# The order of the last block's products, the place of block 0's projection, and the pace of attention tiles 4 to 7 in a fused sliding-window attention and SwiGLU kernel

## The chip, the core and the metric

The kernel runs on one core of a Trainium2 chip. The core has five engines with a queue each: PE (TensorE, matrix products), DVE (VectorE), ACT (ScalarE), POOL (GpSimd, here only an issuer of loads) and SP (SyncE, an issuer of DMAs). They run side by side and meet only at semaphores. Matrix products go from the on-chip memory SBUF into eight accumulator banks, PSUM, of 2 KB per partition; DVE and ACT read them out. Sixteen DMA engines move data between SBUF and the chip's main memory, HBM.

The metric is the device time of one execution in microseconds (us), less is better. A time is the median of several runs. A profile is one execution recorded instruction by instruction; its span runs from the first to the last recorded instruction.

## What is computed

There are 8 batches, 8 heads, 576 tokens and head size 64. Attention is causal with a window of 128 tokens and a linear penalty by distance. Its output, 4608 rows of 512, goes through a gated feed-forward part with 1536 hidden columns:

```python
scores = scale * np.matmul(q, k.transpose(0, 1, 3, 2))
mask = (rel >= 0) & (rel < window)              # window = 128
scores = np.where(mask, scores + bias[None], -1e9)
attn = np.exp(scores - np.max(scores, -1)); attn = attn / (np.sum(attn, -1) + 1e-9)
x = np.matmul(attn, v)          # (8, 8, 576, 64), regrouped to (4608, 512)
g = x @ w_gate
silu = g * (1.0 / (1.0 + np.exp(-g)))
out = (silu * (x @ w_val)) @ w_out
```

## The kernel before

**Attention** works on units: 36 tiles of 128 tokens by all 8 heads, nine for each pair of batches (`units`, line 160). For a tile, `scores` multiplies keys by queries into PSUM (L271, or L306 for the narrow form at the end of a batch), ACT takes the exponential (L277, L310), DVE multiplies with the mask (L283, L314), `weighted` multiplies with the values (L338), DVE divides by the sum (L340, L341) into a tile `x`, and `x_transposed` turns it into `xT` (L364 on PE with a copy on ACT at L368, or a DMA transpose from tile 24 on). Keys and queries are turned by `transposed` (L214, copies on ACT at L217 and DVE at L219) or, from rank 11 on, by a DMA issued from SP (L235). `attention` (L634) is a generator: the scores of tile i+1 are handed out in front of the weighting of tile i, and every `yield` is one attention step; a full tile has nine.

**The feed-forward part** works on nine blocks of 512 rows. For each of twelve hidden slices m, `gate_val` multiplies xT with the gate weights (pg, four matmuls of 512 columns at L390), ACT takes tanh (L404), DVE makes u = (tanh + 1) * pg (L405); then the same with the value weights (pv), and DVE multiplies into hT (L412). The PSUM tiles pg and pv rotate through three banks (`ps_f`, tag "gv"); attention's tiles rotate through four banks (`ps_a`, tag "a"); one more bank (`ps_f`, tag "po") is left for projections.

**The output product** of block 0 is made straight (`project`, L431: four row groups of 12 matmuls at L436, the result scaled on ACT at L440 and stored). For blocks 1 to 8 it is made by a Strassen-like scheme with seven products in place of eight (`strassen`, L481): per row group t (0 or 1) seven products of six matmuls of 256 columns (L502), which accumulate in two 256-column halves X and Y of one PSUM bank, and a separate tile p2. They need sums of quarters of hT (`sums`, L468) and of the weights (`weight_sums`, L453), made on DVE. Each `yield` in `strassen` follows one product. Between products ACT halves X or Y into `p1s`, `u2s`, `p5s`, and DVE finishes the four quarters of the result in `top` and `low`. `store` (L426) issues the DMA of a result from SP; for block 8, whose two half tiles of 64 rows lie in different batches, it issues two, and with `two` the second from ACT.

**The order.** `ffn` (L542) is a generator of feed-forward steps, with their size in steps as its value. `everything` (L709) walks through it, and in front of every step decides how many attention steps to hand out: as many as the running target says (`n_att < target`), and in any case until the tiles that the coming block needs are complete (`done < ready[blk]`; block 1 needs `ready[1] = 8` tiles, that is tiles 4 to 7). In step numbers, block 0 fills steps 1 to 24, block 1 with block 0's projection steps 25 to 60, and each later block 34.5 steps. Attention of tiles 0 to 3 and the first eight steps are put down in program order; behind that a scheduler of the language places the instructions, led by the order in which they were handed out and by its own idea of when each can start. So what is handed out earlier tends to stand earlier, without being bound to.

The last block has nothing beside it: its two row groups `ends[0]` and `ends[1]` are stepped by turns at L569.

Of the kernel before, what the change touches and what calls it, by code (L numbers as in the profile page):

```python
# [10 lines left out]
FP32 = mybir.dt.float32  # L11
# [5 lines left out]
P = 128  # L17
# [4 lines left out]
ALONE = 8  # L22
# [7 lines left out]
LEAD = 6  # L30
PRE = 0
SECOND = 5.5
# [15 lines left out]
def kernel(  # L48
# [10 lines left out]
    nc = tc.nc  # L59
    B, H, S, D = q.shape  # L60
    NTOK, DM = out.shape
# [79 lines left out]
    ps_f = ctx.enter_context(tc.tile_pool(name="ps_f", bufs=3, space=PSUM))  # L141
    ps_a = ctx.enter_context(tc.tile_pool(name="ps_a", bufs=4, space=PSUM))

    def busy(n):

        t_ = ps_f.tile([P, 512], FP32, name="nil", tag="po", bufs=1)
        for _ in range(n):
            nc.tensor.matmul(t_, idle[:, 0:P], idle, start=True, stop=True)
# [265 lines left out]
    def gate_val(n, m):  # L414
        c0 = 384 if (n, m) in acted else 0
        gate(n, m, wide(n, m, "g"), c0)
        yield
        val(n, m, wide(n, m, "v"), c0)
        yield

    def rows_of(n, j):
        if n == 8:
            return [(0, 64, 2 * j * S + 512), (64, 128, (2 * j + 1) * S + 512)]
        return [(0, 128, n * S + j * P)]

    def store(n, j, osb, c0=0, c1=512, two=False):  # L426
        for i, (p0, p1, r0) in enumerate(rows_of(n, j)):
            (nc.scalar if two and i else nc.sync).dma_start(out[r0:r0 + p1 - p0, c0:c1],
                                                            osb[p0:p1, c0:c1])

    def project(n, j, pool, tag, bufs):  # L431
        po = pool.tile([P, DM], FP32, name="po", tag=tag, bufs=bufs)
        for m0 in range(0, NMB, 4):
            for i in range(m0, m0 + 4):
                m = NMB - 1 - i if n == 0 else i
                nc.tensor.matmul(po, hT[n][:, m, j * P:(j + 1) * P], wo_sb[:, m, :],  # L436
                                 start=(i == 0), stop=(i == NMB - 1))
            if m0 + 4 == NMB:
                osb = opool.tile([P, DM], FP32, name="osb", tag="osb")
                nc.scalar.mul(osb, po, 0.5)  # L440
                store(n, j, osb)
            yield
# [5 lines left out]
    HC = DM // 2  # L448
    T1, T2, T3, T4 = (consts.tile([P, HM, HC], FP16, name=f"T{n}") for n in (1, 2, 3, 4))
# [3 lines left out]
    def weight_sums(c):  # L453

        if c == 0:
            one_more.append(supool.tile([P, 1], FP32, name="one", tag="pin", bufs=1))
            nc.vector.memset(one_more[0], 1.0)
        k = slice(2 * c, 2 * c + 2)
        for t_, a, b in ((T1, B12, B11), (T3, B22, B12)):
            nc.vector.scalar_tensor_tensor(out=t_[:, k, :], in0=a[:, k, :], scalar=one_more[0],  # L460
                                           in1=b[:, k, :], op0=ALU.mult, op1=ALU.subtract)
        nc.vector.tensor_sub(T2[:, k, :], B22[:, k, :], T1[:, k, :])
        nc.vector.tensor_sub(T4[:, k, :], B21[:, k, :], T2[:, k, :])
# [17 lines left out]
    def strassen(n, t):  # L481

        h = hT[n]
        A11, A12 = h[:, 0:HM, 0:256], h[:, HM:NMB, 0:256]
        S1, A22 = h[:, 0:HM, 256:512], h[:, HM:NMB, 256:512]
        S2, S3, S4 = hsum[n]
        cols = slice(t * P, (t + 1) * P)
        end = n == NBLK - 1
        pool, tag, bufs = (ps_a, "a", 4) if end and t else (ps_f, "po", 1)
        po = pool.tile([P, 2, HC], FP32, name="po", tag=tag, bufs=bufs)  # L490
        p2 = ps_a.tile([P, HC], FP32, name="p2", tag="a")
        top, low = (opool.tile([P, DM], FP32, name="osb", tag="osb") for _ in range(2))
        if end and t:
            spare = [opool.tile([P, DM], FP32, name="osb", tag="osb") for _ in range(2)]
            p1s, p5s, u2s = spare[0][:, 0:HC], spare[0][:, HC:DM], spare[1][:, 0:HC]
        else:
            p1s, p5s, u2s = (supool.tile([P, HC], FP32, name=i, tag=i, bufs=1)
                             for i in ("p1s", "p5s", "u2s"))

        def product(dst, a, b, start=False):  # L500
            for m in range(HM):
                nc.tensor.matmul(dst, a[:, m, cols], b[:, m, :], start=(start and m == 0),  # L502
                                 stop=(m == HM - 1), skip_group_check=True)

        def half_plus(dst, a, b):
            nc.vector.scalar_tensor_tensor(out=dst, in0=a, scalar=0.5, in1=b,
                                           op0=ALU.mult, op1=ALU.add)

        X, Y = po[:, 0, :], po[:, 1, :]
        product(X, A11, B11, True)  # L510
        nc.scalar.mul(p1s, X, 0.5)
        yield
        product(p2, A12, B21, True)
        half_plus(top[:, 0:HC], p2, p1s)
        yield
        product(X, S2, T2)
        nc.scalar.mul(u2s, X, 0.5)
        yield
        product(Y, S1, T1)
        nc.scalar.mul(p5s, Y, 0.5)  # L520
        yield
        product(X, S3, T3)
        half_plus(low[:, HC:DM], X, p5s)
        if end and t:
            store(n, t + 2, low, HC, DM, True)
        yield
        product(Y, S4, B22)
        half_plus(top[:, HC:DM], Y, u2s)
        store(n, t, top, 0, DM, end)
        yield  # L530
        product(X, A22, T4)
        if end:
            nc.vector.tensor_scalar_mul(low[:, 0:HC], X, 0.5)
        else:
            nc.scalar.mul(low[:, 0:HC], X, 0.5)
        store(n, t + 2, low, 0, HC if end and t else DM, end)
        yield
# [4 lines left out]
    def ffn():  # L542

        for n in range(NBLK):
            if n > 1:
                parts = chain(strassen(n - 1, 0), strassen(n - 1, 1))
            if n == 1:
                for j in range(PRE):
                    for _ in project(0, j, ps_f, "po", 1):
                        yield 1.0  # L550
            for m in range(NMB):
                for half, _ in enumerate(gate_val(n, m)):
                    yield 1.0
                    if n > 1 and 2 * m + half in AT:
                        next(parts)
                        yield 0.75
                if n == 1:
                    if m in (3, 5, 7, 9):
                        for _ in project(0, m // 2 - 1, ps_f, "po", 1):
                            yield 1.0  # L560
                    if m in (4, 6, 8):
                        weight_sums(m // 2 - 2)
                if n > 0 and m >= 9:
                    sums(n, m - 9)
            if n > 1:
                assert next(parts, None) is None

        ends = [strassen(NBLK - 1, t) for t in range(2)]
        for t in 7 * (0, 1):  # L569
            next(ends[t])  # L570
            yield 0.75

# [130 lines left out]
    def progress(steps):  # L703
        total = 0.0
        for size in steps:
            total += size
            yield total

    def everything():  # L709
        nonlocal done  # L710
        base = 0
        busy(WARM)
        with tc.manual_schedule(engines=ENGINES[MANUAL]):
            first_tiles()
            done = FIRST
            steps = progress(ffn())
            while (at := next(steps)) < ALONE:
                if at == 2.0:
                    nc.scalar.copy(idm2, idm)
                if at in (1.0, 3.0, 4.0):  # L720
                    later_masks(2 * (1, 3, 4).index(at) + 2, 2)
        for step in steps:
            if step == MASKS_AT:
                make_masks()

            b1 = 24 + 3 * PRE

            lead = LEAD if done < X_DMA_FROM - 2 else LEAD + 4
            blk = (0 if step + LEAD < b1 else 1 if step + LEAD < 60
                   else min(NBLK - 1, 2 + int((step + lead - 60) // 34.5)))  # L730
            if step < b1:

                target = base + 1.25 * max(0, step - ALONE) + 1.5 * max(0, step - 16)
            elif step < 60:
                target = base + 32 + SECOND * 8 * (step - b1) / (60 - b1)
            else:
                target = base + 32 + SECOND * 8 + (step - 60) * RATE * 8 / 34.5
            while (n_att < target or done < ready[blk]) and att_step():
                pass

    everything()


# [28 lines left out]
```

The softmax here doesn't subtract the row's maximum and nothing guards it: scores larger than these inputs give would overflow.

## Time and profile before

| what | value |
|---|---|
| median of 4 runs | 355.14 us (354.98 to 356.29) |
| the profiled execution, its own time | 354.98 us |
| its span | 353.2 us |
| granted TensorE clock, mean over the span | 0.997 |
| PE busy | 341.2 us of the span |
| DVE busy | 279.4 us |
| ACT busy | 178.1 us |
| matmuls of gate and value, L390 | 115.1 and 114.9 us |
| last twelve matmuls, L502 | 346.98 to 348.45 us |
| last PSUM read, L533 on DVE | 348.49 to 348.91 us |
| last store's issue ends | 349.62 us on SP, 349.92 us on ACT |

The busy time of PE is made of overlapping matmuls, so it says when the engine had something in flight and not that it ran at its peak. A finer measure is the distance between starts: four matmuls of 512 columns in a row take 0.86 us, and where the distance is longer, PE waited. The last 4.3 us of the span hold no matmul.

### The profile page before, as it was taken

To read this page: it belongs to the slowest core of one execution; us is meant where nothing else is said; L and a number is where in the kernel's file an instruction comes from. 1 tells how busy PE (TensorE), PEld (TensorE's weight loads), DVE (VectorE), ACT (ScalarE), POOL (GpSimd) and SP (SyncE) were. 2 spreads that over 40 slices of the span, in tenths; PEclk is the share of its full clock that TensorE was granted. 3 is DMA by queue.
4 is the path that set the end of the run, shared out by engine and by line. 5 is a ranking of instruction groups with operands and counts; after the bars stand their busy time and mean duration, and the time that the engine had idled before them with its cause. 6 is when DMAs were issued, how large, how long until landed. Compare 5 with 4: busy or idle time off the path is not lost.

```text
span 353.2 us, 7294 instructions
## 1 busy us (share of the span) xinstructions
PE 341.2 (97%) x2767; PEld 197.1 (56%) x2767; DVE 279.4 (79%) x619; ACT 178.1 (50%) x357; POOL 108.4 (31%) x134
## 2 busy tenths in 40 slices
PE   7999989999999999999999999999999999999994
PEld 4584444444466646565466555664665566456673
DVE  5568887998777798788986998799878965975772
ACT  2758774655655455565546455455444323332330
POOL 8976582439574365553301110000000000000000
PEclk9999999999999999999999999999999999999998
DMA  9999999999999999999945513211022101101004
GB/s 152 171 180 186 143 183 160 90 156 131 141 180 152 178 169 171 170 157 129 175 53 106 89 35 34 86 34 57 17 75 61 45 2 60 59 2 60 32 30 120
DMA packets 158819, 37.34 MB, mean 106 GB/s; under 512 B 147264, under 2 KB 154304, under 8 KB 158784
## 3 DMA queue, kind: packets, MB, share of 16 engines
q0 software_dynamic: 117280, 18.62, 82.7%
q1 hardware_dynamic: 40816, 17.57, 26.6%
q10 hardware_dynamic: 688, 0.69, 0.6%
q8 instruction: 21, 0.34, 0.4%
q14 instruction: 14, 0.11, 0.1%
HBM read 37.91 MB, written 9.44 MB: 134 GB/s over the span
## 4 chain that ended last, share of the span: by engine, by line
PE 80%; DVE 9%; ACT 7%; issue 2%; ACTq 0%; DVEq 0%
PE pv L390 23%; PE pg L390 23%; PE po L502 16%; PE av L338 4%; PE ps L271 4%; PE p L502 3%; DVE uu L405 2%; ACT exc L310 2%; PE px L364 2%; ACT ex L277 2%; DVE hT L412 2%; PE po L436 2%; ACT tt L404 2%; DVE ex L283 1%; PE pt L214 1%
## 5 line engine op out<-in xcount | busy, mean ns | idle before, releaser
L390 PE MATMUL pv<-xT,wv_sb 128*128 128x512 f16 (+2 forms) x464 | 114.9, 364 | 0.9 <-DVE uu L405 0.5
L390 PE MATMUL pg<-xT,wg_sb 128*128 128x512 f16 (+2 forms) x464 | 115.1, 364 | 0.3 <-DVE xT L366 0.2
L404 ACT ACTIVATE tt<-pg 128x512 f16<-128x512 f32 (+2 forms) x110 | 65.4, 594 | 91.4 <-PE pg L390 87.6
L405 DVE SCALAR_TENSOR_TENSOR uu<-tt,pg 128x512 f16<-128x512 f16 (+2 forms) x109 | 73.4, 674 | 33.0 <-ACT tt L404 32.5
L412 DVE TENSOR_TENSOR hT<-uu,pv 128x512 f16<-128x512 f16 (+2 forms) x110 | 74.0, 673 | 7.3 <-PE pv L390 3.3
L390 PEld LDWEIGHTS <-wv_sb 128*128 128x128 f16 x464 | 42.8, 98 | 37.8 <-issue 3.6
L390 PEld LDWEIGHTS <-wg_sb 128*128 128x128 f16 x464 | 42.7, 98 | 36.8 <-issue 2.8
L277 ACT ACTIVATE ex<-ps 128x512 f16<-128x512 f32 x96 | 50.3, 605 | 14.8 <-PE ps L271 14.8
L181 POOL DMA_DIRECT2D va<-in_v_dram x40 | 34.1, 860 | 45.6 <-PE av L338 37.1
L502 PEld LDWEIGHTS <-hT 128*128 128x128 f16 x384 | 36.4, 98 | 15.9 <-issue 3.4
L187 POOL DMA_DIRECT2D qn<-in_q_dram x39 | 33.3, 859 | 29.8 <-DMA qT<-qn 13.0
L187 POOL DMA_DIRECT2D kn<-in_k_dram x39 | 33.3, 858 | 25.4 <-DMA kT<-kn 21.4
L283 DVE TENSOR_TENSOR ex<-ex,m_reg 128x1024 f16<-128x1024 f16 x42 | 28.8, 688 | 8.2 <-ACT ex L277 8.1
L502 PEld LDWEIGHTS <-S 128*128 128x128 f16 x288 | 27.4, 98 | 12.3 <-issue 2.9
L341 DVE TENSOR_TENSOR x<-av,rec 128x256 f16<-128x256 f32 x72 | 29.2, 420 | 0.7
L502 PE MATMUL po<-T,S 128*128 128x256 f16 x192 | 26.0, 273 | 0.6 <-ACT p5s L520 0.6
L502 PE MATMUL po<-T,hT 128*128 128x256 f16 x192 | 26.1, 272 | 0.4
L310 ACT ACTIVATE exc<-psc 128x512 f16<-128x512 f32 x40 | 21.5, 612 | 4.8 <-PE psc L306 4.8
L338 PEld LDWEIGHTS <-ex 128*128 128x128 f16 x384 | 17.8, 97 | 5.1 <-issue 0.9
L338 PE MATMUL av<-va,ex 128*128 128x65 f16 x384 | 19.9, 193 | 0.4
L271 PE MATMUL ps<-qT,kT 64*128 64x256 f16 x192 | 17.9, 273 | 0.3 <-DVE qT L219 0.2
L368 ACT COPY xT<-px 128x512 f16<-128x512 f16 x20 | 11.7, 585 | 9.6 <-PE px L364 9.5
(82 smaller groups left out, 293.7 us busy)
## 6 DMA issues: line engine op xcount, KB each, us to landing
out_dram<-osb SPq DMA_DIRECT2D x32, 256.0 KB, 2.6
va<-in_v_dram POOLq DMA_DIRECT2D x32, 128.0 KB, 8.1
qn<-in_q_dram POOLq DMA_DIRECT2D x31, 128.0 KB, 7.2
kn<-in_k_dram POOLq DMA_DIRECT2D x31, 128.0 KB, 7.2
wo_sb<-in_moe_w_out_dram POOLq DMA_DIRECT2D x2, 768.0 KB, 9.0
wg_sb<-in_moe_w_gate_dram POOLq DMA_DIRECT2D x4, 256.0 KB, 7.8
wv_sb<-in_moe_w_val_dram POOLq DMA_DIRECT2D x4, 256.0 KB, 8.2
wg_sb<-in_moe_w_gate_dram POOLq DMA_DIRECT2D x1, 512.0 KB, 9.1
```

The costliest lines, as they stand in the source:

```text
L181: nc.gpsimd.dma_start(va[rank][p0:p1, :, 0:D], src)
L187: nc.gpsimd.dma_start(t_[p0:p1], src)
L271: nc.tensor.matmul(two[par][:, j, :], kT[rows, ks, pair, :], qT[rows, p:p + 2, pair, :], start=(j == 0 and not early_tile), stop=(j == 1))
L277: nc.scalar.activation(e[:, o:o + 2, :], banks[q4][par], AF.Exp, scale=scale)
L283: nc.vector.tensor_mul(e[:, o, :], e[:, o, :], reg[:, o, :])
L338: nc.tensor.matmul(av[:, j, :], w, val, start=(n == 0), stop=(n == len(todo) - 1))
L341: nc.vector.tensor_mul(x[:, 4 * half:4 * half + 4, :], av[:, :, 0:D], rec.broadcast_to([P, 4, D]))
L390: nc.tensor.matmul(ps[:, c0:c1], w[:, kb, ms], xT[n][:, kb, c0:c1], start=(kb == 0 and c0 == 0), stop=(kb == NKB - 1 and c1 == 512), skip_ ...
L404: nc.scalar.activation(tt, pg[:, c0:c1], AF.Tanh, scale=0.5)
L405: nc.vector.scalar_tensor_tensor(out=uu, in0=tt, scalar=one if (n, m) == PIN else 1.0, in1=pg[:, c0:c1], op0=ALU.add, op1=ALU.mult)
L412: nc.vector.tensor_mul(hT[n][:, m, c0:c1], acted[(n, m)][1][:, c0:c1], pv[:, c0:c1])
L502: nc.tensor.matmul(dst, a[:, m, cols], b[:, m, :], start=(start and m == 0), stop=(m == HM - 1), skip_group_check=True)
```

## The change

Three things are edited.

1. In the last block, X and Y get a PSUM bank each from the four of attention (`ps_a`), and p2 one of the three "gv" banks. Before, row group 0 had its X and Y in the "po" bank and row group 1 in a bank of `ps_a`. The order of the fourteen products is no longer by turns, but 0 1 0 1 0 0 0 1 0 0 1 1 1 1. Row group 1's upper result is stored in two halves of 256 columns, the first one straight behind its second product, both parts of it from SP; and row group 1's `p5s` is made on DVE in place of ACT.
2. In block 1, the four row groups of block 0's projection are handed out behind slices m = 4, 6, 8, 10 in place of 3, 5, 7, 9.
3. The target of attention steps up to step 24 rises by 1.6 a step from step 8 and 2.75 from step 16 (before 1.25 and 2.75), to 34.8 at step 24 in place of 32; from there it starts at 34 in place of 32 and meets the old line at step 60. And the rule that tiles 4 to 7 be complete takes effect one step ahead of block 1 (`step + 1 < b1`) in place of six.

```diff
@@ strassen
-        pool, tag, bufs = (ps_a, "a", 4) if end and t else (ps_f, "po", 1)
-        po = pool.tile([P, 2, HC], FP32, name="po", tag=tag, bufs=bufs)
-        p2 = ps_a.tile([P, HC], FP32, name="p2", tag="a")
+        if end:
+            X, Y = (ps_a.tile([P, HC], FP32, name="po", tag="a", bufs=4) for _ in range(2))
+            p2 = ps_f.tile([P, HC], FP32, name="p2", tag="gv")
+        else:
+            po = ps_f.tile([P, 2, HC], FP32, name="po", tag="po", bufs=1)
+            X, Y = po[:, 0, :], po[:, 1, :]
+            p2 = ps_a.tile([P, HC], FP32, name="p2", tag="a")
...
-        X, Y = po[:, 0, :], po[:, 1, :]
         product(X, A11, B11, True)
         nc.scalar.mul(p1s, X, 0.5)
         yield
         product(p2, A12, B21, True)
         half_plus(top[:, 0:HC], p2, p1s)
+        if end and t:
+            store(n, t, top, 0, HC)
         yield
         product(X, S2, T2)
         nc.scalar.mul(u2s, X, 0.5)
         yield
-        product(Y, S1, T1)
-        nc.scalar.mul(p5s, Y, 0.5)
+        product(Y, S1, T1, end)
+        if end and t:
+            nc.vector.tensor_scalar_mul(p5s, Y, 0.5)
+        else:
+            nc.scalar.mul(p5s, Y, 0.5)
...
         half_plus(top[:, HC:DM], Y, u2s)
-        store(n, t, top, 0, DM, end)
+        store(n, t, top, HC if end and t else 0, DM, end)
@@ ffn
-                    if m in (3, 5, 7, 9):
-                        for _ in project(0, m // 2 - 1, ps_f, "po", 1):
+                    if m in (4, 6, 8, 10):
+                        for _ in project(0, m // 2 - 2, ps_f, "po", 1):
                             yield 1.0
...
-        for t in 7 * (0, 1):
+        for t in (0, 1, 0, 1, 0, 0, 0, 1, 0, 0, 1, 1, 1, 1):
             next(ends[t])
@@ everything
-            blk = (0 if step + LEAD < b1 else 1 if step + LEAD < 60
+            blk = (0 if step + 1 < b1 else 1 if step + LEAD < 60
...
-                target = base + 1.25 * max(0, step - ALONE) + 1.5 * max(0, step - 16)
+                target = base + 1.6 * max(0, step - ALONE) + 1.15 * max(0, step - 16)
             elif step < 60:
-                target = base + 32 + SECOND * 8 * (step - b1) / (60 - b1)
+                target = base + 34 + (SECOND * 8 - 2) * (step - b1) / (60 - b1)
```

Here `LEAD` is 6, `ALONE` 8, `SECOND` 5.5, `b1` 24 and `base` 0.

## The prediction

> **What bounds the kernel now.** I read the page first, for the engines and their course over the span.
>
> ```profile
> PE 341.2 (97%) x2767; PEld 197.1 (56%) x2767; DVE 279.4 (79%) x619; ACT 178.1 (50%) x357; POOL 108.4 (31%) x134
> ...
> PE   7999989999999999999999999999999999999994
> ```
>
> PE is the bound, and its low slices are the first ones (before 18 us, where the change does nothing), the sixth (44 to 53 us) and the last. So an edit of order can win only what PE loses there. Next I read the busy time by stretches, with borders at what the change touches: the attention of tiles 4 to 8 up to block 1's first matmul at 56.11, block 1, and the end. Columns are the stretch, its length, then busy time of PE, PEld, DVE, ACT, POOL (with counts), clock, DMA share and GB/s.
>
> ```profile
> 36.00:44.00 8.00, 7.90 (x71) 3.92 (x69) 6.82 (x15) 5.67 (x12) 4.62 (x7) 1.00 2.05 139
> 44.00:47.50 3.50, 3.50 (x28) 1.78 (x26) 3.40 (x9) 2.11 (x5) 3.50 (x6) 1.00 1.22 184
> 47.50:55.50 8.00, 6.70 (x95) 3.99 (x95) 6.41 (x16) 6.15 (x14) 4.57 (x6) 1.00 1.81 180
> 60.00:70.00 10.00, 10.00 (x77) 4.76 (x76) 9.76 (x21) 5.69 (x11) 3.62 (x5) 1.00 1.46 99
> 70.00:80.00 10.00, 9.79 (x66) 4.37 (x65) 10.00 (x24) 6.27 (x12) 4.18 (x5) 1.00 1.91 156
> 349.00:353.20 4.20, 0.00 (x0) 0.00 (x0) 0.00 (x0) 0.00 (x0) 0.00 (x0) 0.73 0.52 170
> ```
>
> PE idles 1.30 us between 47.5 and 55.5 and next to nothing around it; DVE is full from 60 to 80; the last 4.2 us belong to the DMAs. The chain of waits inside that window says what PE waits for (start, length, what):
>
> ```profile
> 48.52 0.99 ACT exc L310 x2
> ...
> 49.53 0.69 DVE exc L314
> 50.22 0.16 DVE rec L340 x2
> 50.38 0.40 DVE x L341
> ...
> 50.83 0.28 PE px L364 x2
> 51.11 0.37 PE psc L306 x8
> 51.49 1.07 ACT exc L310 x2
> 52.56 0.48 ACT xT L368
> 53.04 1.00 ACT exc L310 x2
> ```
>
> This is the serial course of tiles 6, 7 and 8 through ACT and DVE, with hardly a feed-forward matmul between its steps: the old rule completes tiles 4 to 7 from step 18 on, and block 0 has little left to put between them. At the other end I read the DMA issues of the last stores, the first pair (window 346.2 to 347) and the last pair (349.0 to 349.3):
>
> ```profile
> out_dram<-osb SPq DMA_DIRECT2D x1, 64.0 KB, 2.0
> out_dram<-osb ACTq DMA_DIRECT2D x1, 64.0 KB, 2.3
> ...
> out_dram<-osb SPq DMA_DIRECT2D x1, 64.0 KB, 2.7
> out_dram<-osb ACTq DMA_DIRECT2D x1, 64.0 KB, 2.8
> ```
>
> The same 64 KB take 0.5 to 0.7 us longer in the last pair, because 1 MB is pressed into the DMA engines within 3 us.
>
> **The change part by part.** *Attention of tiles 4 to 8.* The built order of the changed kernel differs from the old one from 30.6 us (matmul 295 on each side) to matmul 811 (102.5 us before); behind that PE's order is the same up to the last block, so whatever is won or lost carries through. I laid the new order out by hand from 30.63 us, each instruction behind the one ahead of it, what it reads, and the read that frees its bank. Durations are from the timeline: 0.216 us for a matmul of 512 columns (four in 0.86), 0.22 for four transposes, 0.24 for a weighting half, 0.49 for an ACT exponential or copy, 0.61 for a DVE operation of 512 or a mask (0.68 less the overlap), 0.35 for L341, and 0.2 from a matmul group's end to its reader. What it gives:
> - Removed: in the old order one matmul (0.22 us) stands between tile 6's weighting and its transposes (px). That matmul should end at 50.00; px starts at 50.83 and, for the second half, at 51.76 in place of 51.23: 0.83 + 0.53 of waiting. In the new order eight matmuls stand there (1.73 us). The new chain is two mask operations, two reciprocals and two L341, ready some 2.4 us behind the first weighting half: a wait of about 0.4 is left, none for the second half.
> - Added: tile 5 loses that cover, four matmuls behind its weighting where there were nine. A tanh stands ahead of tile 6's exponentials, and the first weighting half needs the bank that the first of these frees: 0.5 more. Its x then comes late for px, and px's banks for the transposes behind: 0.2. Tile 5's own queries are copied behind one more DVE operation: 0.3.
> - The rest (scores of tile 8 and its weighting, which wait for ACT's copy and exponentials in both orders) I get at 0.75 now and 0.55 before.
>
> By this, block 1's first matmul comes at 55.75 in place of 56.11, with 10 of the projection's matmuls done in place of 8: 0.36 + 2 x 0.216 = **0.8 us won**. The bounds: no more than the idle PE of 36 to 55.5 in the rows plus the gaps too short for them (0.10 + 1.30 + about 0.3) = 1.7 won; and if the removed waits come back in full while the added ones stay, 1.0 lost. I take 0.8.
>
> *Block 0's projection.* The 48 matmuls (L436) are the same. The scheduler pulled the first ones into the attention of tile 8 already (matmul 479 before, 487 now). What moves is the rest: at matmul 680, 36 of them were done before and 32 are now, so 4 x 0.216 = 0.86 us of PE work without DVE is late, and one slice's DVE work comes earlier, while DVE is full (10.00 of 10.00). ACT's reads and SP's four stores move along; POOL's loads, which the new order also shuffles on POOL and SP, were ahead: the waiting lists hold no wait of PE for a load. PE idles 0.21 from 70 to 80, so 0.2 can be won; if the late 0.86 us is all waited for, 0.9 is lost. I take 0: pg and pv have three banks, worth 2.6 us of matmuls, as cover.
>
> *The last block.* Eighty-four matmuls at 109 ns are 9.16 us, and they take 9.3 (338.98 to the last nominal end at 348.29): 0.1 can be won. A product's reader ends 1.28 us behind its start, and PE goes on 0.06 later; two products last 1.31. In the old order every product waits for a read two products back, since X and Y share a tile. In the new one only three do (S3T3 of group 0, the last two of group 1, of which one reads `p5s` on DVE); S1T1 now stands alone. I take 0 here, bounds 0.1 won to 0.3 lost (three waits of 0.1).
>
> *The stores.* Before, 1 MB is issued from 346.28 to 349.16. Now a 128 KB half goes at about 342.3, group 0's two results at 345.6 and 346.3, and the last three halves 0.65 us apart. The issues cost SP and ACT about 0.55 each and stand 0.65 apart, so they don't pile up; the lanes that they reuse landed long before. The last pair (2.7 and 2.8) should then go towards the first pair (2.0 and 2.3): 2.8 - 2.35 = **0.45 won**, bounds 0 and 0.7. In the built program the last landing also moves from the third of SP's eight final waits to the fifth or sixth; these go by in 0.06 us each in the trace: **0.12 won**.
>
> The Trainium skill (DMA: Bandwidth & Descriptors, under "Measured (HBM→SBUF, 128 partitions, SWDGE, issued from GpSimd)") speaks against pieces like these: it asks for DMAs of 1 MiB and calls those under 64 KB bound by their descriptors. The row is against it here, since 64 KB landed after 2.0 us alone and 2.7 in the crowd. The page's own fit of 2.0 us plus bytes over 436 GB/s would make the last pair an estimated 2.15 us, and the gain 0.65 in place of 0.45.
>
> *Sum*, on the profiled execution (354.98 us, of which the span is 353.2 and 1.8 lie around it): 0.8 + 0 + 0 + 0.45 + 0.12 = 1.37, so 353.6. Its run lies 0.16 below the median of 355.14, so against the median I forecast **353.8 us**.
>
> **The rivals.** *Only the end gains.* The waits of tiles 6 to 8 move to tile 5 and to block 1 and PE ends where it did: 355.14 - 0.57 = 354.6. For it: ACT and DVE must do the same serial work, and my list of added waits is as long as that of the removed ones. Against it: DVE has 1.6 us free between 47.5 and 55.5 and another 1.2 between 36 and 44.
>
> *DVE in block 1 becomes the bound.* Place: 60 to 80 us, where DVE has 0.24 us free in 20. If the late projection and the attention steps that now stand in block 1's first slices put DVE further behind than the three banks cover (2.6 us), PE waits for every slice until DVE catches up behind 80. The price is the DVE work of two slices that arrive without cover, each L405 + L412 = 1.35: 2.7 us, less 0.57 at the end: 355.14 + 2.1 = 357.2; half of that gives 355.9. For it: the row with 10.00. Against it: the change leaves DVE's amount of work in block 1 nearly the same, and weight sums stay where they were.
>
> *The change doesn't do what it says.* The scheduler orders behind step 8, so a pace handed out need not be the pace built. The built order does show the spread (eight matmuls in place of one ahead of px), so I hold this for spent but for the projection, which hardly moves; it is within the first rival.
>
> **How the numbers follow.** The forecast case has 0.62, its own range 352.8 (both main bounds nearly full: 355.14 - 1.7 - 0.6) to 354.5. Only the end gains: 0.20. DVE becomes the bound: 0.18. About 0.3%, 1.07 us, is what a measurement tells from no change, so faster means under 354.07: most of the first case, 0.52, and 0.03 of the second; the same holds 0.10 of the first, 0.17 of the second and 0.02 of the third; slower the remaining 0.16. The range 352.7 to 355.8 takes in the first two cases and the milder part of the third.
>
> **What would show it.** Right: busy PE in the stretch before block 1 up by about 0.8 us, tile 6's px without a wait of 0.7, block 1's first matmul near 55.8, the seventh product's matmuls 0.8 us earlier than at 346.98, and last landings near 2.3 us after issue. Wrong: waits of PE for DVE between 60 and 80 us, tile 5's weighting waiting more than 0.7, or the last pair still at 2.7.

## The result, and the profile after

The changed kernel takes 355.06 us in the median of 52 runs; the kernel before, run beside it 77 times, takes 355.91. The ratio of the means is 0.9971, with a 95% interval of 0.9965 to 0.9978, or 1.03 us of 355.14. (The medians differ by 0.85 only, since the changed kernel's runs fall in two groups, see below.) So it is faster, by three quarters of the 1.37 us that the forecast had, and its 353.8 is 0.3 us too low on the old median (355.14 - 1.03 = 354.1). Three of the four runs shown before had been at the low end of the kernel's own spread.

The profiled execution took 355.06 us, its span is 353.285 (before 353.203 of 354.98). So this pair of profiles shows no gain at all, while 52 runs do. That is what has to be explained. First the busy shares and PE's forty slices on the page:

```profile
span 353.3 us, 7299 instructions
...
PE 341.0 (97%) x2767; PEld 197.9 (56%) x2767; DVE 279.3 (79%) x620; ACT 177.1 (50%) x356; POOL 108.4 (31%) x134
...
PE   7999998999999999999999999999999999999995
```

The sixth slice (44 to 53 us) is at nine tenths or more now, and the seventh (53 to 62) is at eight instead. The stretches say the same in microseconds (columns as in the prediction):

```profile
47.50:55.50 8.00, 7.01 (x82) 3.90 (x80) 6.40 (x16) 5.42 (x11) 4.62 (x6) 1.00 1.81 180
55.50:57.50 2.00, 1.15 (x10) 0.72 (x10) 0.61 (x2) 0.57 (x1) 0.88 (x1) 1.00 2.45 154
60.00:70.00 10.00, 10.00 (x76) 4.57 (x75) 9.84 (x22) 5.29 (x10) 4.08 (x5) 1.00 1.99 138
70.00:80.00 10.00, 10.00 (x68) 4.53 (x68) 9.98 (x22) 6.80 (x14) 6.70 (x10) 1.00 2.19 152
```

PE gains 0.31 us of busy time between 47.5 and 55.5 (6.70 before) and is idle for 0.85 of the next two (busy 1.15 of 2.00; 1.98 before). From 60 to 80 it is full beside a full DVE, so the rival of DVE did not come. The list of PE's waits from 30 to 58 us (total, times, longest) names the loser:

```profile
PE po L436 <- DMA wo_sb<-in_moe_w_out_dram: 1.1, 1, 1.1
PE ps L271 <- DVE qT L219: 0.5, 1, 0.5
PE av L338 <- ACT ex L277: 0.3, 1, 0.3
PE px L364 <- DVE x L341: 0.3, 1, 0.3
PE psc L306 <- ACT xT L368: 0.3, 1, 0.3
```

Before, the same list had px with 1.0 us in two waits and ps with 0.2, and nothing else. So one of px's two waits is gone and the other is smaller, as forecast; ps waits longer, two small waits (av, psc) are new, and one that was not forecast tops the list: block 0's projection waits for the second half of the output weights. The chain of waits over 48 to 58 us shows that wait as a load of 11 us, with PE behind it (start, length, what):

```profile
45.14 11.17 DMA wo_sb<-in_moe_w_out_dram
56.31 0.04 issue
56.35 0.38 PE po L436
...
57.71 0.45 PE pg L390 x2
```

The timeline of PE says what it cost, in starts: the matmul after 54.84 should stand at 55.06.

```profile
54.84 0.38 PE L436 MATMUL po<-wo_sb,hT 128*128 128x512 f16 x1
56.35 0.38 PE L436 MATMUL po<-wo_sb,hT 128*128 128x512 f16 x1 [1.13 <-DMA wo_sb<-in_moe_w_out_dram]
```

At the end the last stores land sooner (issues behind 349.65 us; the second ACT store there is the last to land, at 352.19):

```profile
out_dram<-osb ACTq DMA_DIRECT2D x2, 64.0 KB, 2.3
out_dram<-osb SPq DMA_DIRECT2D x1, 64.0 KB, 2.1
```

Three distances sum up the end. The last 84 matmuls take 9.08 us from first to last start in place of 9.19; from the last matmul's start to the last landing it is 3.26 us in place of 3.81; from there to the end of the span 1.09 in place of 1.22. Together 0.79 us.

### The profile page after: what moved, and what is told of

It reads as the page before. It is cut to its first block, busy times and chain, and to the rows that moved or that the text cites. A ratio compares the mean times of both kernels' runs of the same rounds, so it can differ in the third digit from the quotient of the medians.

```text
span 353.3 us, 7299 instructions
## 1 busy us (share of the span) xinstructions
PE 341.0 (97%) x2767; PEld 197.9 (56%) x2767; DVE 279.3 (79%) x620; ACT 177.1 (50%) x356; POOL 108.4 (31%) x134
## 4 chain that ended last, share of the span: by engine, by line
PE 72%; DMA 11%; DVE 6%; ACT 4%; POOL 4%; issue 3%; DVEq 0%; ACTq 0%; POOLq 0%
PE pv L390 21%; PE pg L390 21%; PE po L506 16%; DMA wg_sb<-in_moe_w_gate_dram 4%; PE av L338 4%; DMA wo_sb<-in_moe_w_out_dram 3%; DMA va<-in_v_dram 3%; PE p L506 3%; PE ps L271 3%; PE po L436 2%; DVE hT L412 2%; DVE uu L405 1%; ACT ex L277 1%; POOL va L181 1%; PE px L364 1%
```

## The experiments

In all runs the time outside the span is mostly 1.7 to 2.1 us, at times up to 3.5, whatever the kernel. So the spans of all runs (the profiled one included) are the finer measure, and they already say something: 23 runs of the changed kernel span 351.8 to 352.5 us, 30 span 353.0 to 354.3, and none lies between.

**The two halves of the change.** The first kernel has only the edits of `strassen` and of the order of the fourteen products, the second only those of `ffn`'s projection and of `everything`.

```diff
 tail_only
-            pool, tag, bufs = (ps_a, "a", 4) if end and t else (ps_f, "po", 1)
+            X, Y = (ps_a.tile([P, HC], FP32, name="po", tag="a", bufs=4) for _ in range(2))
...
-        for t in 7 * (0, 1):
+        for t in (0, 1, 0, 1, 0, 0, 0, 1, 0, 0, 1, 1, 1, 1):
 mid_only
-                    if m in (3, 5, 7, 9):
+                    if m in (4, 6, 8, 10):
...
-                target = base + 1.25 * max(0, step - ALONE) + 1.5 * max(0, step - 16)
+                target = base + 1.6 * max(0, step - ALONE) + 1.15 * max(0, step - 16)
```

> Only the last block's part of the change (banks, order of the fourteen products, half store, p5s on DVE); pace and projection as before. Theory A (the end gives its full gain whatever the middle does): the profile of the changed kernel shows 0.11 us less for the last 84 matmuls, 0.55 us less from the last matmul to the last landing, 0.13 us less behind it; so 0.79 us faster than the kernel before, ratio 0.9978, and both its fastest and its slowest runs shift alike. Rival B (the gain at the end was the smaller part, most of the 1.03 us came from the pace): 0.3 us or less, ratio 0.999 or above.

> Only the pace of tiles 4 to 7 and the later projection; the last block as before. Theory A: PE gains 0.4 us by the first product of block 1 where the second half of wo_sb is there in time, and nothing or a loss where PE waits for it as in the profile of the changed kernel (1.29 us between two projection matmuls at 54.84 us); so runs fall in two groups about 1.2 us apart as those of both kernels do, and the ratio is 0.9985 to 1.0005. Rival B: 0.8 us as forecast, ratio 0.9978.

The last block's part alone took 354.73 us, ratio 0.9975 (0.9958 to 0.9992); the middle alone 356.37, ratio 1.001 (0.9998 to 1.0022). So the last block's part brings the gain (theory A) and the middle, on this stream of loads, none. The spans of the middle alone fall in two groups about 1.4 us apart, three of twelve at 353.0 to 353.3 and nine at 354.2 to 355.0, as theory A had it. Both profiles wait for the weights. First the last block's part, then the middle alone, the top of each list of PE's waits:

```profile
PE px L364 <- DVE x L341: 1.0, 2, 0.7
PE po L436 <- DMA wo_sb<-in_moe_w_out_dram: 0.8, 1, 0.8
```

```profile
PE po L436 <- DMA wo_sb<-in_moe_w_out_dram: 1.5, 1, 1.5
PE ps L271 <- DVE qT L219: 0.4, 1, 0.4
```

The first of them has the old order of attention, whose profile before had no such wait. So the wait is not a thing of the new order alone.

**The weights one load earlier.** The load of `wo_sb[0:6]` is issued straight behind that of `wo_sb[6:12]`, ahead of the keys and queries of ranks 9 and 10, in both kernels.

```diff
     nc.gpsimd.dma_start(wo_sb[:, 6:12, :], wo2[:, 6:12, :])
+    nc.gpsimd.dma_start(wo_sb[:, 0:6, :], wo2[:, 0:6, :])
     load_qk(9)
     load_qk(10, "q")
-    nc.gpsimd.dma_start(wo_sb[:, 0:6, :], wo2[:, 0:6, :])
```

> The changed kernel with one load moved: the half of wo_sb that holds rows 0 to 5 is issued straight behind the other half, ahead of the keys and queries of ranks 9 and 10. The orders of PE, DVE and ACT are the same as in the changed kernel. Theory A (the late landing of this load parts the runs into two groups and takes back the gain in the middle): the wait of 1.29 us is gone, the runs are one group near the lower one, median 353.9, ratio to the kernel before 0.994 to 0.9955. Rival C (the two groups come from elsewhere, for instance from the first loads): two groups as now, ratio 0.997.

> The kernel before with the same load moved as in the run above it. Theory A: its two groups (near 355.2 and 356.2) become one near 355.1, ratio 0.997 to 0.9985, and the profile shows no wait of PE for wo_sb. Rival C: two groups as before, ratio 1.000. If A holds here and in the changed kernel, the difference of these two is the change without the load: 1.2 us.

The changed kernel so took 354.4 us (0.997, 0.9953 to 0.9986), ten of twelve spans at 352.3 to 352.8: the upper group is nearly gone, as theory A had it, but the lower one is 0.3 to 0.5 us higher, so the time is the one of rival C. Its profile waits for the queries of rank 10, which the weights now stand ahead of:

```profile
PE pt L214 <- DMA qn<-in_q_dram: 0.3, 1, 0.3
```

The kernel before took 356.25 (1.0016, 0.9999 to 1.0032): no gain, against theory A. The loads land one behind another (in the profile before, the three between the two halves of the weights landed 0.8 to 1.0 us apart), so in the changed kernel the move made another load the late one. For the kernel before that isn't shown: its profile (span 353.5) waits for no load, and why its spans stayed at 353.5 to 355.2, with one of 357.3, is open.

**Rank 8's values behind them.** What isn't needed soon is rank 8's values. In this edit both halves of the weights stand in front and the values behind rank 10's queries, in three kernels: changed, before, and the last block's part alone. The order of PE, DVE and ACT is each kernel's own.

```diff
-    load(8)
+    load_qk(8)
     nc.gpsimd.dma_start(wo_sb[:, 6:12, :], wo2[:, 6:12, :])
+    nc.gpsimd.dma_start(wo_sb[:, 0:6, :], wo2[:, 0:6, :])
     load_qk(9)
     load_qk(10, "q")
-    nc.gpsimd.dma_start(wo_sb[:, 0:6, :], wo2[:, 0:6, :])
+    load_v(8)
     load_v(9)
```

> The changed kernel with both halves of the output weights loaded right behind rank 8's queries and keys, and rank 8's values behind rank 10's queries (the order of the matmuls, of DVE and of ACT is the changed kernel's). Theory A (the middle wins about 0.4 us where loads are out of the way, and the changed kernel's two groups of spans come from the last part of the weights' second half): no wait of PE for the weights and none of more than 0.2 us for the queries of rank 10, since these keep their place; block 1's first matmul near 56.3 with the start of block 1 of the changed kernel's good runs, spans in one group at 352.0 or under, 3.1 us under the kernel before in the median of time it should show 0.995 to 0.996. Theory B (the middle wins nothing even so, the tail is all): the spans go to 352.5 to 353.0, as with the last block's part alone, and some other wait of 0.3 to 0.5 us takes the place of that for the weights.

> The kernel before with the same move of the loads. Theory A (the kernel before doesn't wait for its weights in most runs): 0.999 to 1.001, spans with a median of 353.8 to 354.1. Theory B (the broad spread of its spans, 353.1 to 354.8, is also made by late loads): the spread becomes narrow, 353.0 to 353.6, and the ratio 0.998.

> The last block's part of the change alone, with the same move of the loads. Theory A: span 0.8 us under that of the kernel before with this move (0.55 from the last matmul to the last landing, 0.13 behind it, 0.11 in the last 84 matmuls), and 0.4 us over the changed kernel with this move. Theory B: no difference to the changed kernel with this move (within 0.15 us).

| kernel, loads moved | median, us | ratio to before (95%) | spans, us |
|---|---|---|---|
| changed | 353.98 | 0.9945 (0.9927 to 0.9963) | 351.8 to 352.3 |
| last block's part alone | 354.48 | 0.9957 (0.9941 to 0.9973) | 352.1 to 353.3 |
| before | 355.57 | 0.9988 (0.9974 to 1.0002) | 353.2 to 353.9 |

Theory A holds for the changed kernel: it has one group of spans now, block 1's first matmul stands at 56.28, and at 0.9945 it is better than both kernels of this study. In its list of PE's waits the weights are gone and the other four are as they were:

```profile
PE ps L271 <- DVE qT L219: 0.4, 1, 0.4
PE av L338 <- ACT ex L277: 0.3, 1, 0.3
PE px L364 <- DVE x L341: 0.3, 1, 0.3
PE psc L306 <- ACT xT L368: 0.3, 1, 0.3
```

The spans of the kernel before went from 353.1 to 354.8 (median 354.1) to 353.2 to 353.9: its longer half is gone too, which speaks for theory B, though B had 353.6 as the upper end and the ratio's interval still holds 1. And the middle, which was worth nothing above, is now worth some: 0.5 us by the medians, 0.6 by the spans' medians (352.0 against 352.6). A better measure is the first Strassen product (all matmuls before it are the same work in each kernel) counted from PE's 291st matmul, where the orders are still alike: 67.31 us for the kernel before with moved loads, 67.00 for the changed one, so 0.31 won. The measure repeats well: it is 67.32 in the four profiles of the kernel before that waited for no load, and 66.94 to 67.00 in three kernels with the changed middle and moved loads. The two products start here, before first:

```profile
96.73 0.60 PE L502 MATMUL po<-wo_sb,hT 128*128 128x256 f16 x4
96.45 0.82 PE L506 MATMUL po<-wo_sb,hT 128*128 128x256 f16 x6
```

(The profile of the last block's part alone has 67.49; it waits 0.3 for the queries of rank 10, and this is part of the 0.6.)

**The weights later.** To see that the wait does set the end, `wo_sb[0:6]` is loaded behind rank 10's keys in the changed kernel.

```diff
-    nc.gpsimd.dma_start(wo_sb[:, 0:6, :], wo2[:, 0:6, :])
     load_v(9)
     load_qk(10, "k")
+    nc.gpsimd.dma_start(wo_sb[:, 0:6, :], wo2[:, 0:6, :])
```

> The changed kernel with the load of the second half of the output weights issued behind the keys of rank 10, one load later: the suspected wait made longer. Theory A (the weights' last part sets block 1's start): block 0's first projection matmul waits for the weights in every run, 0.8 to 1.0 us longer than the 1.29 us of the changed kernel's profile (2.0 to 2.3), the two groups of spans become one at 353.8 to 354.6, ratio to the kernel before 0.999 to 1.001. Theory B (the wait in the profile is a place where slack shows, and the spans are set later, by block 1): the spans stay where the changed kernel's are, ratio 0.996 to 0.998.

```profile
PE po L436 <- DMA wo_sb<-in_moe_w_out_dram: 2.2, 1, 2.2
```

The wait grew from 1.1 to 2.2 us, and the time to 357.2 us, ratio 1.0032 (1.0013 to 1.005): the wait and the direction are theory A's, but the ratio is above its 1.001. It had not foreseen a second group of spans, 355.7 to 356.3 beside 353.8 to 354.8. The profile fell in that group, and in it PE ran for 3.4 us at half its clock behind the long wait (the column before the last two is the granted clock):

```profile
58.00:62.00 4.00, 4.00 (x17) 1.68 (x16) 0.47 (x2) 1.18 (x2) 2.62 (x3) 0.57 2.43 155
```

So part of the 1.0032 is this clock and not the load. Whether all six long runs had it isn't known, since one was profiled.

**The parts of the last block.** On the base with moved loads, the early half store is taken away (`v8_no_half`), or the products go by turns again (`v8_old_turns`).

```diff
 v8_no_half
-        if end and t:
-            store(n, t, top, 0, HC)
...
-        store(n, t, top, HC if end and t else 0, DM, end)
+        store(n, t, top, 0, DM, end)
 v8_old_turns
-        for t in (0, 1, 0, 1, 0, 0, 0, 1, 0, 0, 1, 1, 1, 1):
+        for t in 7 * (0, 1):
```

> The changed kernel with the moved loads, but row group 1's upper result stored whole again (the early half store is taken away; 128 KB of the last 1 MB goes out 5.6 us later than it did). Theory A (the last landing is set by how many bytes crowd in behind the last products): from the last matmul's start to the last landing 3.4 to 3.7 us, where the changed kernel has 3.06 to 3.31 and the kernel before 3.81 to 4.18; the last 84 matmuls stay at 9.08. Theory B (the order of the products brings it, since group 0's 512 KB are gone before): 3.1 to 3.3, no difference.

> The changed kernel with the moved loads and the early half store, but with the fourteen products by turns again. Theory A (bytes that crowd in): group 0's 512 KB go out within 2 us of the last matmul again, so 3.5 to 3.9 us from the last matmul to the last landing; and if the 0.11 us in the last 84 matmuls come from the banks, these stay at 9.08, if from the order, at 9.19. Theory B (the half store is what counts): 3.1 to 3.3.

| profiles | last 84 matmuls, us | last matmul to last landing, us | from there to the end, us |
|---|---|---|---|
| old last block (8 profiles) | 9.19 to 9.20 | 3.81 to 4.19, mean 4.01 | 1.21 to 1.23 |
| new last block (10 profiles) | 9.08 | 3.06 to 3.31, mean 3.15 | 1.09 to 1.11 |
| without the early half store | 9.08 | 3.61 | 1.21 |
| products by turns | 9.06 | 3.76 | 1.11 |

Theory A holds in both. The 0.11 us of the matmuls don't come from the order or the half store, since they stay in both; that leaves the banks, and `p5s` on DVE, which both kernels keep too. The starts show where they were lost. In the profile before, three of the 84 matmuls start late (0.149, 0.188 and 0.130 us behind the one ahead of them in place of 0.109), held up by ACT's read for `p5s` and twice by DVE's read for a result; in the new last block only one does (0.132). So at most the first, 0.04 us, can belong to `p5s`. The landing needs both the order and the half store; either taken away gives half a microsecond back, because more bytes are then in flight behind the last matmul. The issues of the last microsecond show it, first without the half store, then by turns:

```profile
out_dram<-osb ACTq DMA_DIRECT2D x1, 128.0 KB, 2.8
out_dram<-osb SPq DMA_DIRECT2D x1, 64.0 KB, 2.5
out_dram<-osb ACTq DMA_DIRECT2D x1, 64.0 KB, 2.7
```

```profile
out_dram<-osb SPq DMA_DIRECT2D x1, 128.0 KB, 2.9
out_dram<-osb ACTq DMA_DIRECT2D x1, 128.0 KB, 3.1
out_dram<-osb SPq DMA_DIRECT2D x1, 64.0 KB, 2.7
out_dram<-osb ACTq DMA_DIRECT2D x1, 64.0 KB, 2.6
```

The 128 KB stores that the change had sent earlier, or had cut in two, are back, and the 64 KB ones behind them take 2.5 to 2.7 us in place of 2.0 to 2.3. The last 0.12 us come and go with the half store alone. In time, both kernels are between (0.9965, 0.9951 to 0.9979; 0.9966, 0.9953 to 0.9979).

**The parts of the middle.** On the same base, block 0's projection is put back (`v8_pace`), or the pace is (`v8_proj`).

```diff
 v8_pace
-                    if m in (4, 6, 8, 10):
-                        for _ in project(0, m // 2 - 2, ps_f, "po", 1):
+                    if m in (3, 5, 7, 9):
+                        for _ in project(0, m // 2 - 1, ps_f, "po", 1):
 v8_proj
-            blk = (0 if step + 1 < b1 else 1 if step + LEAD < 60
+            blk = (0 if step + LEAD < b1 else 1 if step + LEAD < 60
...
-                target = base + 1.6 * max(0, step - ALONE) + 1.15 * max(0, step - 16)
+                target = base + 1.25 * max(0, step - ALONE) + 1.5 * max(0, step - 16)
...
-                target = base + 34 + (SECOND * 8 - 2) * (step - b1) / (60 - b1)
+                target = base + 32 + SECOND * 8 * (step - b1) / (60 - b1)
```

> The changed kernel with the moved loads, block 0's projection where it was before: the pace alone. Theory A (the pace makes the middle's gain): first Strassen product within 0.15 us of the changed kernel with moved loads (96.45) and spans at 351.8 to 352.2. Theory B (the projection's later place makes it): spans at 352.4 to 352.8, like the last block's part alone with moved loads (median 352.6).

> The changed kernel with the moved loads and the old pace: only block 0's projection moved, besides the last block's part. Theory A (the pace makes the gain, the projection nothing, as forecast): first Strassen product at 96.7 to 97.0, spans at 352.3 to 352.7, the 0.83 and 0.53 us waits of tile 6's transposes back. Theory B: spans at 351.8 to 352.2.

The times are 354.27 us (0.9958, 0.9944 to 0.9972) and 354.42 (0.9963, 0.9946 to 0.998), with medians of the spans at 352.35 and 352.3: both between the last block's part alone (352.6) and the whole (352.0). So neither theory is right: the second kernel shows the waits and the first Strassen product (97.00) that A gave it, but the pace doesn't make the gain either, since its kernel has that product at 97.07. The positions tell why, all from the 291st matmul, with moved loads:

| kernel | block 1's first matmul, us | projection matmuls done by then | first Strassen product, us |
|---|---|---|---|
| before | 26.56 | 8 | 67.31 |
| pace alone | 26.84 | 10 | 67.29 |
| projection alone | 26.54 | 8 | 67.17 |
| both | 26.84 | 10 | 67.00 |

The pace wins 0.43 - 0.28 = 0.15 us ahead of block 1 (two matmuls more, 0.28 later), and block 1 takes 0.13 of it back if the projection stays. The projection's place wins 0.12 inside block 1 alone and 0.16 with the pace, and it takes both for 0.31. These are differences of one profile a kernel. The profile of the projection alone has tile 6's waits back, as expected:

```profile
PE px L364 <- DVE x L341: 1.0, 2, 0.7
PE ps L271 <- DVE qT L219: 0.2, 1, 0.2
```

**Further executions of both kernels.** They ask where each kernel's spread comes from; each is a single profiled execution.

> The kernel before once more, one profiled execution. Theory A (the runs of the kernel before are spread over 353.1 to 354.9 by the load of the output weights too): a span over 353.9 shows a wait of PE for the weights of 0.5 us or more ahead of block 1, and a span under 353.6 shows none over 0.3 us. Theory B (its spread comes from the last landings, 3.81 to 4.18 us behind the last matmul in four profiles, or from the start): a span over 353.9 without such a wait.

> The kernel before a third time; the same two theories. A: with a span over 353.9 a wait of PE for the weights of 0.5 us or more, with a span under 353.6 none over 0.3 us. B: a long span without such a wait, from the last landings or the start.

> The changed kernel once more. Theory A: a span of 352.5 or less shows no wait of PE for the weights over 0.3 us, a span of 353.0 or more shows one of 0.9 to 1.4 us; in the first case the second half of the weights has all its sixteen parts by about 55.2 us and the 16 KB instruction packet runs beside another part of the transfers or later, in the second one part lands a microsecond behind the rest, on the engine that carried the packet. Theory B: the two groups differ elsewhere (start or last landing by a microsecond).

> The changed kernel a third time; the same two theories. A: span 352.5 or less without a wait of PE for the weights over 0.3 us, span 353.0 or more with one of 0.9 to 1.4 us. B: groups that differ at the start or at the last landing.

> The kernel before once more, for its longer runs. Theory A (late weights in these): a span over 354.1 shows a wait of PE for the weights or for the queries of rank 10 of 0.4 us or more between 52 and 57 us; a span under 353.9 shows none over 0.3. Theory B (start and last landings alone, as in the three profiles so far): a span over 354.1 whose first Strassen product comes 67.3 us behind the kernel's 291st matmul, as in those.

> The kernel before once more, the same two theories. A: a span over 354.1 with a wait of PE for the weights or for the queries of rank 10 of 0.4 us or more between 52 and 57 us. B: a span over 354.1 whose first Strassen product comes 67.3 us behind the 291st matmul.

| execution | span, us | 16th part of the weights lands, us | the 15 others by, us | reader's matmul, us | PE's wait in starts, us |
|---|---|---|---|---|---|
| changed, profile | 353.3 | 56.31 | 55.01 | 56.35 | 1.29 |
| changed, `after_look2` | 353.3 | 56.43 | 54.94 | 56.47 | 1.6 |
| changed, `after_look3` | 352.0 | 55.26 | 54.96 | 55.30 | 0.44 |
| before, profile | 353.2 | 54.99 | 54.78 | 55.49 | none |
| before, `before_look2` | 353.3 | 54.91 | 54.67 | 55.36 | none |
| before, `before_look3` | 353.8 | 54.82 | 54.75 | 55.72 | none |
| before, `before_look4` | 354.3 | 56.66 | 55.39 | 56.71 | 1.28 |

(The parts are the sixteen completions that the trace records for one transfer.) For the changed kernel theory A holds: the upper group waits over a microsecond, the lower one under half of one. First `after_look3`, then `before_look4`, the line of the weights in the lists of PE's waits:

```profile
PE po L436 <- DMA wo_sb<-in_moe_w_out_dram: 0.3, 1, 0.3
```

```profile
PE po L436 <- DMA wo_sb<-in_moe_w_out_dram: 1.1, 1, 1.1
PE px L364 <- DVE x L341: 1.0, 2, 0.7
```

So the kernel before has the late weights too, in one of the two longer executions that were profiled. Between 353.2 and 353.8 its spread comes from elsewhere, as theory B had it (start 0.36 us apart, last landing 3.81 to 4.19). `before_look5`, 355.5 us, waits for no weights: its 291st matmul came 2.1 us late, behind a stretch of 3.4 us with PE at half clock (the granted clock from 8 to 14 us is 0.72), and from there to the first Strassen product it takes 67.32 us, as theory B had it.

## Why the prediction was right and where it was wrong

**The attention of tiles 4 to 8, 0.8 us won: wrong, 0.15 ahead of block 1 and 0.31 with the projection's part, where the loads are out of the way.** The parts that were listed were nearly right: with loads moved, tile 6's 0.83 and 0.53 fell to 0.46 and 0, tile 5's weighting waited 0.48 (0.5 in the list) and the scores behind its queries 0.23 more than before (0.3). Only they don't add up to 0.8. The prediction's own list is 0.96 removed against 0.5 + 0.2 + 0.3 and another 0.2 added, so nothing or a slight loss; the 0.8 was read from where a hand-laid order ended, and the two were never set against each other. The runs showed block 1's first matmul 0.28 us later and not 0.36 earlier; which step of the hand-laid order made it end too early isn't known, since only its end was given.

**"POOL's loads were ahead: the waiting lists hold no wait of PE for a load": the step that failed.** The prediction so put the loads at nothing. A list of waits tells what PE waited for, not by how little it missed a wait. In the profile before, the second half of the weights, issued at 44.86, landed at 54.99, and its reader stood at 55.49: 0.5 us of slack. The first line is the load (window 44.9 to 45.0; KB, us to landing), the second its reader:

```profile
wo_sb<-in_moe_w_out_dram POOLq DMA_DIRECT2D x1, 768.0 KB, 10.1
55.49 0.59 PE L436 MATMUL po<-wo_sb,hT 128*128 128x512 f16 x2
```

The change brings that reader forward by 0.55 (from 25.95 us behind the 291st matmul to 25.40 with loads moved), so the slack is gone. A landing that comes later by chance then costs PE time: in `after_look3` the weights landed 25.85 us behind the 291st matmul, 0.4 later than in the profile before (25.44), which the reader of the kernel before, at 25.95, would not have felt. So even a prompt load costs the changed kernel 0.26 us at the first Strassen product (67.26 from the 291st matmul in `after_look3`, against 67.00), and a late one 1.12 to 1.35 (68.12 and 68.35 in the two others). The Trainium skill (DMA: Bandwidth & Descriptors, "Why a DMA increments its semaphore by 16 and not by 1") says that only the full count of sixteen means that all data has landed. The runs agree: fifteen parts were there by 55.01 us, and PE stood until the last, at 56.31.

What this took back: by the means of all spans, the moved loads are worth 0.85 us to the changed kernel (352.90 to 352.05) and 0.40 to the kernel before (354.02 to 353.62). The difference, 0.45, is what the change lost to the loads; by the spread of these spans it is uncertain by 0.3. So it takes back about what the middle part wins (0.31), which fits the 1.001 of the middle alone.

**Block 0's projection, 0: nearly right.** Alone it won 0.12 us in block 1, within its bounds; on top of the pace, whose gain block 1 otherwise takes back, it is worth 0.29 (67.29 to 67.00), over the 0.2 that could be won. The list of PE's waits from 60 to 100 us is empty in the profile after. So the rival of DVE as the bound is out.

**The last block's PE, 0: 0.11 us won, the upper bound,** from the banks, but for the 0.04 at most that may be `p5s`.

**The stores, 0.45 us: right in mechanism, too small by half.** The landing came 0.86 us sooner (mean 4.01 to 3.15). Both ends of the term were off. The last pair took 2.7 and 2.8 us in the profile that was read, but 2.8 to 3.1 and 2.9 to 3.2 in the seven others of the old last block; and it went to 2.0 to 2.3, under the 2.35 that the sum had taken as the goal. The upper bound of 0.7 was too low as well, since it was made from that one execution. The estimate from the Trainium skill's fit (DMA: Bandwidth & Descriptors, "Anatomy of one DMA — SWDGE (gpsimd) path"), 2.15 us, is what the last pair came to, though the page gives the fit for DMAs from GpSimd and these go from SP and ACT. The page's rule for large DMAs spoke the wrong way here: putting the early 64 KB pieces back into 128 KB stores cost half a microsecond (3.61 against 3.12 us). What that run changes is the time of sending as well as the size, so it doesn't show that small pieces move faster.

**The final waits, 0.12 us: right,** 1.22 to 1.10.

**The sum.** Measured it is 0.11 + 0.86 + 0.12 = 1.09 from the end, 0.31 from the middle, 0.45 lost to the loads: 0.95, beside 1.03 from the ratio. The forecast had 0.8 from the middle, which brought nothing or a slight loss on its own loads (0.31 - 0.45), and 0.57 from the end, which brought 1.09. That 1.37 came as near as it did is luck: two wrong terms leaned opposite ways. The first rival, that only the end gains, is nearest to what happened; its time of 354.6 was high for the same stores. A gain of 1.03 us is just under the 1.07 that was taken for the least that a measurement tells; with 52 and 77 runs the interval, 0.78 to 1.24, tells it from nothing.

## What to carry to other kernels

- Before work is pulled forward, take for each operand it reads the time between its landing and its reader: the list of waits is silent about a slack of 0.5 us, and that was all there was. Then move the load with the work, in front of what is needed later; moved in front of something needed sooner, as with rank 10's queries here, it only changed the name of the wait.
- When waits are both removed and added, set the list of them against the end of the laid-out order. If the two differ, neither is a forecast.
- At the end of a kernel, spread the bytes and not just the issues: here order and an early half store together were worth 0.86 us, where PE's better order in the middle was worth 0.31, and a bound made from one execution was too narrow.

## What the hardware showed that was not expected

One of the sixteen parts of a 768 KB load came 1.3 to 1.5 us behind the other fifteen in three of the seven executions in the table (1.2 and 1.8 in the profiles of the two halves of the change), and within 0.3 us of them in the other four, with the load's issue between 44.9 and 45.5 us in all. In that stretch an instruction transfer of 16 KB ran among the loads:

```profile
q8 instruction: 1, 0.02, 0.8%
```

It took 0.9 to 1.0 us and began at 54.09 to 54.24 us in all five late profiles (the two halves of the change among them). But it began at 54.18 in the prompt execution of the changed kernel and at 54.26 in `before_look2`, which was prompt too, and the trace doesn't say which of the sixteen engines carried it. So it may be the cause where it meets the last part on one engine; that is argued, not shown, and it wasn't tried.

In two executions PE ran at half its clock for 3.4 us, once at the start and once (in `after_wo_late`) from about 0.8 us behind the end of an idle time of 2.22 us. At the start of the first, `before_look5`, the longest idle times of PE were 1.2 us, as in these lines of its list of PE's waits:

```profile
PE nil L148 <- DVE kT L112: 1.2, 1, 1.2
PE pt L207 <- DMA stage<-in_q_dram: 1.2, 1, 1.2
PE pt L214 <- DVE qT L208: 0.8, 1, 0.8
```

The start of `after_wo_late` has the same three waits with the same lengths, and its granted clock from 8 to 14 us is 1.00. So the length of the idle times alone doesn't decide; what does stays open. The shorter waits for the weights, up to 1.6 us in starts, were followed by full clock in every profile here. The Trainium skill (TensorE: Matmul & The Clock Gate, "Why this matters for your kernels") puts the pause that brings the clock down at about 3 us; in these two executions it came down with no idle time longer than 2.22 and 1.2 us ahead of it.
